# Windowed attention and soft mixture of experts on one core: three-row constants for the distance ramp, an earlier maximum in round 1, seven unused products

## The chip, the cores and the metric

The kernel runs on one core of a Trainium2 chip. The metric is the device time of one execution in microseconds. The core has five engines that run side by side, each with its own queue of instructions: TensorE (PE in the profile, with its weight loads listed apart as PEld), VectorE (DVE), ScalarE (ACT), GpSimd (POOL) and SyncE (SP), which here only issues transfers.

## The reference

Attention over a window of 128 positions with a penalty that grows with distance, then a soft mixture of experts over all tokens:

```python
# q, k, v: batch 8, heads 8, positions 576, head size 64
scores = scale * q @ k.T
bias = slopes * (-|i - j|)
scores = where((i - j >= 0) & (i - j < 128), scores + bias, -1e9)
attn = softmax(scores);  x = attn @ v            # 4608 tokens x 512
logits = x @ phi                                 # 32 slots: 8 experts x 4
slot_input = softmax(logits, over tokens).T @ x
slot_out = relu(slot_input @ w1[e]) @ w2[e]      # per expert, 512 -> 1024 -> 512
out = softmax(logits, over slots) @ slot_out
```

## The kernel before

**Rounds.** Attention is cut into 72 groups: per batch four tiles of 128 queries in two halves of the heads each, and a last tile of 64 queries in one piece. The loop over `i` (L726) is one round per group, and in a round the engines work on different groups. Everything stands under an order written out by hand, so each engine executes its instructions in the order of the code.

**Scores of a group** (`scores`, L235 on). Two banks of products are filled. The first four products (L252) write the distance ramp: a constant `pair_of` as weights against a constant `ramp` as moving operand, 384 columns in bf16. Only three of their rows hold anything; the operands have 64 rows each, of which 61 are zero, so that these products have the shape 64*64 (rows*columns of the array that they occupy) like the products of queries and keys after them. Those (L261) are fp32, sixteen in a round, and add on top of the ramp. Four of either kind sit in the four quarters of the array at the same time.

**Softmax of a group.** `merge` (L277, DVE) folds the two windows into one by a mask, `rowmax` (L291, DVE) takes the negated maximum, `bias` (L295, DVE) scales it, `expo` (L354, ACT) makes the four exponentials with their sums, `total` (L300) adds a small constant to the sums (on POOL, in round 2 on DVE), `inverse` (L304, DVE) takes the reciprocal, `normalise` (L308, DVE) multiplies. `softmax_front(new, old)` orders this for the group whose scores have just come and the group before it.

**After that.** `flip` (L369, PE, shape 64*128) transposes the normalised weights, `split` (L375 ACT, L381 and L383 POOL) copies and masks them, `values` (L405, PE, shape 128*64) multiplies with v, `x_store` (L419, DVE) copies out; `x_flip` (L428), `logits` (L446) and what follows feed the mixture. In round `i` PE has: flip of an older group, values of a still older one, scores of group `i+1`, then pieces of the mixture. `scores(i+1)` overwrites the bank that `expo(i-1)` read and waits for it.

**The first rounds differ.** Round 0 has only scores and softmax, in two halves. In round 1, `softmax_front` treats group 0 as `first`: the total (POOL) and the reciprocal (DVE) of group 0 come ahead of the maximum of group 1, half of the normalising is done on ACT (`normalise_first`, L313) and half on DVE. The first flip of weights is that of group 0, in round 2, after `scores(2)`.

**The start.** Six warm-up products (L225, 512 columns of bf16) run on a zeroed tile while the first loads are under way. SP issues keys of tile 0 (L185), then, once DVE has cleared `ramp` and `pair_of` (L204, L205), four small transfers of constants (L217, L218), and later the other loads; ACT issues the three first loads of queries (L181). A transfer's semaphore is one of eight, given out in turn, so the ninth transfer is issued when the first has landed.

Of the kernel before, what the change touches and what calls it, by code (L numbers as in the profile page):

```python
# [10 lines left out]
F32 = mybir.dt.float32  # L11
F32R = mybir.dt.float32r
BF16 = mybir.dt.bfloat16
# [11 lines left out]
P = 128  # L25
# [10 lines left out]
WIN = P + KB  # L36
# [7 lines left out]
FLAG = 3  # L44
# [15 lines left out]
def slide(ap):  # L60
    return bass.AP(ap.tensor, ap.offset, [list(ap.ap[0]), [KB, 2], [1, WIN]])
# [10 lines left out]
def tile_attn_softmoe(  # L72
# [13 lines left out]
    nc = tc.nc  # L86

    cpool = ctx.enter_context(tc.tile_pool(name="cpool", bufs=1))
# [16 lines left out]
    ln = lne[:, :, 0:NS]  # L105
    acc = cpool.tile([P, DM], F32, name="acc")
    kq = cpool.tile([P, 3 * UW], F32, name="kq")
    ramp = cpool.tile([P, 2, 2 * P], BF16, name="ramp")
    pair_of = cpool.tile([P, 2, P], BF16, name="pair_of")
    area = cpool.tile([P, 20, HW], F32, name="area")  # L110

    kall = kq[:, 0:NPAIR * S].rearrange("p (n j w) -> p n j w", n=NB, j=NPAIR)
    qs = [kq[:, NPAIR * S + 2 * P * i:NPAIR * S + 2 * P * i + 2 * P] for i in range(3)]
    half = [slice(64 * par, 64 * par + 64) for par in range(2)]

    def halves(i):
        return area[:, i].rearrange("p (u w) -> p u w", u=4)
# [25 lines left out]
    st = {}  # L143
# [54 lines left out]
    v_taken = []  # L198

    with tc.manual_schedule(engines=ORDERED):  # L200
        warm = area[:, 2].bitcast(BF16)[:, 0:512]
        nc.vector.memset(warm, 0.0)
        nc.vector.memset(low, LOW)
        nc.vector.memset(ramp, 0.0)  # L204
        nc.vector.memset(pair_of, 0.0)  # L205
        nc.vector.memset(fine[:, 10:11], -1.0)
        nc.gpsimd.memset(mask, 1.0)
        for c in range(2):
            rows = slice(KB * c, KB * c + KB)
            nc.gpsimd.affine_select(  # L210
                mask[rows, 0], mask[rows, 0], [[-1, KB]], ALU.is_ge, 0.0, base=0, channel_multiplier=1)
            nc.gpsimd.affine_select(
                mask[rows, 1], mask[rows, 1], [[1, KB]], ALU.is_gt, 0.0, base=0, channel_multiplier=-1)
        load_k(0, 0)
        load_q(0, nc.scalar)
        for par in range(2):
            nc.sync.dma_start(ramp[64 * par:64 * par + 3], slopes[par, :, 2 * P:])  # L217
            nc.sync.dma_start(pair_of[64 * par:64 * par + 3], slopes[par, :, 0:2 * P])  # L218
        load_q(1, nc.scalar)
        load_q(2, nc.scalar)  # L220
        load_k(0, 1)
        tiny = work.tile([P, 1], F32, tag="nm", name="tiny")
        nc.scalar.activation(tiny, low, AF.Exp)
        for i in range(WARM):
            nc.tensor.matmul(free[i % 4], lhsT=warm[:, 0:P], rhs=warm, start=True, stop=True)  # L225
        nc.gpsimd.memset(lgm, LOW)
        nc.gpsimd.memset(lne[:, :, NS:NS + 1], EPS)
        nc.gpsimd.memset(area[:, 3, 0:P], 1.0)
        nc.gpsimd.affine_select(
            unit_r, area[:, 3, 0:P], [[1, P]], ALU.is_equal, 0.0, base=0, channel_multiplier=-1)  # L230
        load_v()
        nc.scalar.dma_start(cst[:, P:], cstd)
        nc.scalar.dma_start(phi, phid)
        for t in range(2, NT):
            load_k(0, t)  # L235

    def scores(i):
        b, t, g = groups[i]
        if i == 0:
            parts = [pq[:, 0], ps_1.tile([P, 4 * P], F32, tag="xp", name="s4_0")]  # L240
        else:
            parts = [s4s[i % 2][:, 2 * par:2 * par + 2].rearrange("p u w -> p (u w)") for par in range(2)]
        qt = qs[i % 3].rearrange("p (j w) -> p j w", w=width(t))
        second = WIN if t < 4 else 2 * P
        for par, rows in enumerate(half):
            if t < 4:
                dst, src = parts[par][:, 0:2 * WIN], slide(ramp[rows, g])
            else:
                dst, src = parts[par].rearrange("p (u w) -> p u w", u=2)[:, :, 0:WIN], ramp[rows, :, 0:WIN]
            for jj in range(2):  # L250
                strip = slice(KB * jj, KB * jj + KB)
                nc.tensor.matmul(  # L252
                    dst[strip], lhsT=pair_of[rows, int(t == 0), strip], rhs=src, start=True, stop=False)
        for u in range(2):
            h, hp = (u, g) if t < 4 else (0, u)
            skip = max(2 * (1 - t) - h, 0)
            m0 = 2 * (t - 1) + h
            for par, rows in enumerate(half):
                for jj in range(2):
                    j = 2 * hp + jj  # L260
                    nc.tensor.matmul(  # L261
                        parts[par][KB * jj:KB * jj + KB, second * u + KB * skip:second * u + WIN],
                        lhsT=qt[rows, jj if t < 4 else j, KB * h:KB * h + KB], rhs=kall[rows, m0 + skip:m0 + 3, j],
                        start=False, stop=(u == 1))
        st[groups[i]] = {"parts": parts, "s4": s4s[i % 2].rearrange("p (a u) w -> p a (u w)", a=2)}
# [31 lines left out]
    def total(key, us, eng=None):  # L297
        if "rs" not in st[key]:
            st[key]["rs"] = work.tile([P, 4], F32, tag="rs", name="rs", bufs=3)
        (eng or nc.vector).tensor_scalar(  # L300
            st[key]["rs"][:, us], st[key]["sm"][:, us], EPS, 1.0, op0=ALU.add, op1=ALU.mult)

    def inverse(key, us):
        nc.vector.reciprocal(st[key]["rs"][:, us], st[key]["rs"][:, us])  # L304

    def normalise(key, us):
        p4, rs = st[key]["p4"][:, us], st[key]["rs"][:, us]
        nc.vector.tensor_tensor(p4, p4, bc(rs, 2, P), op=ALU.mult)  # L308

    def normalise_first(key, us):  # L310
        p4 = st[key]["p4"]
        for u in range(4)[us]:
            nc.scalar.mul(p4[:, u], p4[:, u], st[key]["rs"][:, u:u + 1])  # L313

    fillers = []

    def filler():
# [3 lines left out]
    def softmax_front(new, old):  # L321
        first, eager = number[old] == 0, 0 < number[old] < EAGER
        late = number[new] > SKIP
        if number[new] > SKIP + 1:
            normalise(groups[number[old] - 1], ALL)
        merge(new)
        filler()
        if not eager:
            total(old, ALL, nc.gpsimd)
        if first:  # L330
            inverse(old, ALL)
            normalise_first(old, LO)
        rowmax(new, ALL)
        filler()
        if not first and not eager:
            inverse(old, ALL)
        filler()
        bias(new, ALL)
        if eager:
            total(old, ALL)  # L340
            inverse(old, ALL)
        filler()
        if not late or number[new] == n - 1:
            normalise(old, HI if first else ALL)

    def expo(key, us=ALL):
        s = st[key]
# [11 lines left out]
    def flip(key, us=ALL, to=None, pair=None):  # L359
        s = st[key]  # L360
        if to is not None:
            s["pt"] = to.rearrange("p u (r w) -> p u r w", r=2)
            for u in range(4)[us]:
                nc.tensor.transpose(to[:, 2 * (u % 2) + u // 2], s["p4"][:, u], ident)
            return
        s["pt"] = (pq_p if pair is None else pair).rearrange("p r (u w) -> p u r w", u=4)
        for u in range(4)[us]:
            for r, rows in enumerate(half):
                nc.tensor.transpose(s["pt"][:, 2 * (u % 2) + u // 2, r], s["p4"][rows, u], ident[rows, rows])  # L369
# [350 lines left out]

    turn, ready = [0], {}

    with tc.manual_schedule(engines=ORDERED):
        scores(0)
        loads(0)
        for i in range(n):  # L726
            new = groups[i]
            run("pre", i)
            if i:
                softmax_front(new, groups[i - 1])  # L730
            else:
                for us in (LO, HI):
                    merge(new, us)
                    rowmax(new, us)
                    bias(new, us)
                    expo(new, us)
            near = int(i < SKIP)
            if i + near >= FLAG and i != SKIP:
                flip(groups[i + near - FLAG])
                split(groups[i + near - FLAG])  # L740
            run("act", i)
            if i + near >= LAG and i != SKIP:
                values(groups[i + near - LAG])
                after_values(i, groups[i + near - LAG])
            if i + 1 < n:
                scores(i + 1)
            if i + 1 < n - 1:
                loads(i + 1)
            if i == n - 1:
                run("pe", i)  # L750
                x_keep(last, 2)
            if i:
                expo(new)
            run("pe", i)
            load_weights_at(i)
            run("dve", i)
# [321 lines left out]
```

## Time and profile before

| | us |
|---|---|
| median of 3 runs (lowest, highest) | 277.69 (276.69, 278.99) |
| the profiled execution, whole | 277.36 |
| its span, first to last instruction | 275.4 |
| PE busy | 253.3 (92%) |
| VectorE busy | 214.4 (78%) |
| ScalarE busy | 189.5 (69%) |
| GpSimd busy | 108.5 (39%) |
| mean granted clock of TensorE, share of full | 0.979 |

Busy shares are means over stages: the start (to about 18 us), the attention rounds (to about 212 us) and the experts with the output (to the end). Matmuls are pipelined, so that the distance from the start of one block of products to the start of the next says more than the printed durations. The chain of the profile is the sequence of work that ended last, followed backwards.

### The profile page before, as it was taken

To read this page: it belongs to the slowest core of one execution; us is meant where nothing else is said; L and a number is where in the kernel's file an instruction comes from. 1 tells how busy PE (TensorE), PEld (TensorE's weight loads), DVE (VectorE), ACT (ScalarE), POOL (GpSimd) and SP (SyncE) were. 2 spreads that over 40 slices of the span, in tenths; PEclk is the share of its full clock that TensorE was granted. 3 is DMA by queue.
4 is the path that set the end of the run, shared out by engine and by line. 5 is a ranking of instruction groups with operands and counts; after the bars stand their busy time and mean duration, and the time that the engine had idled before them with its cause. 6 is when DMAs were issued, how large, how long until landed. Compare 5 with 4: busy or idle time off the path is not lost.

```text
span 275.4 us, 11691 instructions
## 1 busy us (share of the span) xinstructions
PE 253.3 (92%) x4589; PEld 176.5 (64%) x4589; DVE 214.4 (78%) x549; ACT 189.5 (69%) x778; POOL 108.5 (39%) x221
## 2 busy tenths in 40 slices
PE   6599999989999999899998999999999899999980
PEld 2366676767667677667766766667767433777750
DVE  2779998997997899699799899789896556674450
ACT  2868878897897788778888889778977301154450
POOL 3025735480675276328526551656755001000000
PEclk9779999999999999999999999999999999999996
DMA  6834557888897979887879988787577799977997
GB/s 167 291 88 144 156 165 254 257 285 275 256 304 250 308 238 309 278 273 233 270 239 335 315 266 275 270 283 221 160 256 236 244 334 384 408 282 257 332 362 273
DMA packets 36478, 72.49 MB, mean 263 GB/s; under 512 B 4380, under 2 KB 14792, under 8 KB 36424
## 3 DMA queue, kind: packets, MB, share of 16 engines
q1 hardware_dynamic: 35704, 71.25, 77.9%
q8 instruction: 36, 0.59, 0.9%
q10 hardware_dynamic: 720, 0.51, 0.6%
q14 instruction: 18, 0.15, 0.2%
HBM read 62.30 MB, written 9.44 MB: 261 GB/s over the span
## 4 chain that ended last, share of the span: by engine, by line
PE 59%; DVE 15%; ACT 11%; POOL 6%; issue 5%; DMA 2%; ACTq 0%; POOLq 0%; DVEq 0%
PE xp L405 14%; PE s L261 9%; ACT area L354 8%; PE op L917 5%; PE hp L878 5%; PE pq L369 4%; PE s L252 4%; DVE s L291 4%; PE lp L446 4%; DVE area L308 4%; PE po L942 3%; POOL area L383 3%; PE pq L428 3%; DVE s L277 2%; POOL area L381 2%
## 5 line engine op out<-in xcount | busy, mean ns | idle before, releaser
L354 ACT ACTIVATE area<-s,nb 128x128 f32<-128x128 f32 x286 | 101.9, 378 | 24.6 <-DVE nb L295 22.6
L405 PE MATMUL xp<-area 128*64 128x128 f32 (+1 forms) x1104 | 72.9, 271 | 2.3 <-POOL area L383 1.7
L354 ACT ACTIVATION_READ_ACCUMULATOR area<-s,nb 128x1 f32 x286 | 61.9, 216 | 0.0
L405 PEld LDWEIGHTS xp<-area 128*64 128x64 f32 x1104 | 54.2, 137 | 9.9 <-POOL area L383 5.0
L308 DVE TENSOR_TENSOR area<-area,rs 128x512 f32<-128x512 f32 (+1 forms) x73 | 58.1, 796 | 0.6
L261 PE MATMUL s<-kq 64*64 64x192 f32 (+2 forms) x1144 | 56.2, 311 | 1.0 <-issue 0.8
L291 DVE TENSOR_REDUCE s<-s 128x4 f32<-128x512 f32 (+1 forms) x72 | 50.0, 694 | 2.2
L375 ACT COPY area<-pq 128x512 f32<-128x512 f32 (+1 forms) x72 | 42.5, 593 | 10.4 <-PE pq L369 8.9
L383 POOL TENSOR_SCALAR_AFFINE_SELECT area<-area 128x512 f32<-128x512 f32 (+1 forms) x57 | 45.4, 797 | 3.9
L381 POOL TENSOR_SCALAR_AFFINE_SELECT area<-area 128x512 f32<-128x512 f32 (+1 forms) x57 | 37.7, 662 | 21.8 <-ACT area L375 20.7
L300 POOL TENSOR_SCALAR rs<-sm 128x4 f32<-128x4 f32 x70 | 15.0, 215 | 77.4 <-ACT area L354 71.4
L261 PEld LDWEIGHTS s<-kq 64*64 64x64 f32 x1144 | 39.4, 135 | 5.1 <-issue 1.1
L369 PE MATMUL pq<-unit_r,area 64*128 64x64 f32 x560 | 31.9, 233 | 3.2 <-ACT area L313 2.2
L277 DVE COPY_PREDICATED s<-cst,s 128x256 f32<-128x256 int32 (+1 forms) x72 | 30.1, 418 | 2.4 <-PE s L261 2.4
L369 PEld LDWEIGHTS pq<-unit_r,area 64*128 64x128 f32 x560 | 23.4, 140 | 13.2 <-issue 3.9
L419 DVE COPY area<-xp 128x512 f32<-128x512 f32 (+1 forms) x38 | 24.2, 636 | 6.4 <-PE xp L405 5.9
L252 PE MATMUL s<-ramp,pair_of 64*64 64x384 bf16 x286 | 26.1, 350 | 3.3 <-ACT area L354 2.4
L437 ACT COPY area<-pq 128x512 f32<-128x512 f32 x34 | 20.4, 600 | 0.6 <-PE pq L428 0.6
L428 PEld LDWEIGHTS pq<-unit_r,area 64*128 64x128 f32 x272 | 11.0, 137 | 14.6 <-issue 12.1
L252 PEld LDWEIGHTS <-pair_of 64*64 64x64 bf16 x288 | 9.3, 103 | 16.1 <-issue 11.8
L428 PE MATMUL pq<-unit_r,area 64*128 64x64 f32 x272 | 15.7, 234 | 0.6 <-ACT area L375 0.4
L944 ACT COPY ob<-po 128x512 f32<-128x512 f32 x20 | 11.3, 587 | 6.1 <-PE po L942 5.6
(145 smaller groups left out, 264.5 us busy)
## 6 DMA issues: line engine op xcount, KB each, us to landing
w<-w SPq DMA_DIRECT2D x53, 512.0 KB, 5.5
out<-ob SPq DMA_DIRECT2D x36, 256.0 KB, 3.5
kq<-q_t SPq DMA_DIRECT2D x69, 128.0 KB, 3.9
area<-v_n SPq DMA_DIRECT2D x33, 256.0 KB, 5.1
kq<-k_t SPq DMA_DIRECT2D x32, 256.0 KB, 4.1
area<-w SPq DMA_DIRECT2D x8, 512.0 KB, 7.1
kq<-w SPq DMA_DIRECT2D x3, 512.0 KB, 6.8
kq<-k_t SPq DMA_DIRECT2D x8, 128.0 KB, 3.9
```

What stands on the lines that cost most here:

```text
L252: nc.tensor.matmul(dst[strip], lhsT=pair_of[rows, int(t == 0), strip], rhs=src, start=True, stop=False)
L261: nc.tensor.matmul(parts[par][KB * jj:KB * jj + KB, second * u + KB * skip:second * u + WIN], lhsT=qt[rows, jj if t < 4 else j, KB * h:KB ...
L277: nc.vector.copy_predicated(to, keep, of)
L291: nc.vector.tensor_reduce(st[key]["mx"], merged(key, us), axis=AX.X, op=ALU.max, negate=True)
L308: nc.vector.tensor_tensor(p4, p4, bc(rs, 2, P), op=ALU.mult)
L354: nc.scalar.activation(s["p4"][:, u], src, AF.Exp, bias=s["nb"][:, u:u + 1], scale=SCALE, accum_out=s["sm"][:, u:u + 1],)
L369: nc.tensor.transpose(s["pt"][:, 2 * (u % 2) + u // 2, r], s["p4"][rows, u], ident[rows, rows])
L375: nc.scalar.copy(pa[:, us].rearrange("p u (r w) -> p u r w", r=2), s["pt"][:, us])
L381: nc.gpsimd.affine_select(prev, own, [[-step, m], [0, 4], [-1, KB]], ALU.is_gt, 0.0, base=-i0, channel_multiplier=1)
L383: nc.gpsimd.affine_select(own, own, [[step, m], [0, 4], [1, KB]], ALU.is_ge, 0.0, base=i0, channel_multiplier=-1)
L405: nc.tensor.matmul(xp[D * par:D * par + D, j, 0:w], lhsT=v_slot[b, t - 1 + ph][:, D * h:D * h + D], rhs=src[:, :, par, i] if t < 4 else sr ...
L428: nc.tensor.transpose(xq[:, j, r], x[rows, j], ident[rows, rows])
```

## The change

- One tile `slp` takes the place of `ramp` and `pair_of`. The constants are loaded into rows 0 to 2 and 64 to 66 with one transfer each, issued as the first transfers of SP and of ACT, ahead of the keys and queries; the two clearing memsets and the four transfers behind them go. The ramp's products use these three rows alone (`three[par]`) in place of 64, in every round.
- In round 1 the maximum and `bias` of group 1 come ahead of the reciprocal of group 0, and DVE does the whole normalising of group 0; `normalise_first` goes.
- Six products without use run on PE ahead of the first flip of weights (in round 2) and one behind it, from the zeroed tile of the warm-up, which moves from `area[:, 2]` to `area[:, 15]` so that it is still there.

```diff
-    ramp = cpool.tile([P, 2, 2 * P], BF16, name="ramp")
-    pair_of = cpool.tile([P, 2, P], BF16, name="pair_of")
+    slp = cpool.tile([P, 6 * P], BF16, name="slp")
+    pair_of = slp[:, 0:2 * P].rearrange("p (a w) -> p a w", a=2)
+    ramp = slp[:, 2 * P:].rearrange("p (a w) -> p a w", a=2)
...
+    three = [slice(64 * par, 64 * par + 3) for par in range(2)]
...
-        warm = area[:, 2].bitcast(BF16)[:, 0:512]
+        for par, eng in enumerate((nc.sync, nc.scalar)):
+            eng.dma_start(slp[three[par]], slopes[par])
+        warm = area[:, 15].bitcast(BF16)[:, 0:512]
...
-        nc.vector.memset(ramp, 0.0)
-        nc.vector.memset(pair_of, 0.0)
...
-        for par in range(2):
-            nc.sync.dma_start(ramp[64 * par:64 * par + 3], slopes[par, :, 2 * P:])
-            nc.sync.dma_start(pair_of[64 * par:64 * par + 3], slopes[par, :, 0:2 * P])
...
-                dst, src = parts[par][:, 0:2 * WIN], slide(ramp[rows, g])
+                dst, src = parts[par][:, 0:2 * WIN], slide(ramp[three[par], g])
...
-                    dst[strip], lhsT=pair_of[rows, int(t == 0), strip], rhs=src, start=True, stop=False)
+                    dst[strip], lhsT=pair_of[three[par], int(t == 0), strip], rhs=src, start=True, stop=False)
...
-        if first:
-            inverse(old, ALL)
-            normalise_first(old, LO)
         rowmax(new, ALL)
...
         if eager:
             total(old, ALL)
+        if eager or first:
             inverse(old, ALL)
         filler()
         if not late or number[new] == n - 1:
-            normalise(old, HI if first else ALL)
+            normalise(old, ALL)
...
+    def busy(k):
+        to = ps_1.tile([P, 512], F32, tag="mi", name="busy")
+        for _ in range(k):
+            nc.tensor.matmul(to, lhsT=warm[:, 0:P], rhs=warm, start=True, stop=True)
...
+                if i + near == FLAG:
+                    busy(6)
                 flip(groups[i + near - FLAG])
+                if i + near == FLAG:
+                    busy(1)
```

More of the change, by code (lines that the diff above doesn't have):

```diff
@@ L246, in scores @@
             if t < 4:
-                dst, src = parts[par][:, 0:2 * WIN], slide(ramp[rows, g])
+                dst, src = parts[par][:, 0:2 * WIN], slide(ramp[three[par], g])
             else:
-                dst, src = parts[par].rearrange("p (u w) -> p u w", u=2)[:, :, 0:WIN], ramp[rows, :, 0:WIN]
+                dst, src = parts[par].rearrange("p (u w) -> p u w", u=2)[:, :, 0:WIN], ramp[three[par], :, 0:WIN]
             for jj in range(2):
@@ L308, in normalise @@
         nc.vector.tensor_tensor(p4, p4, bc(rs, 2, P), op=ALU.mult)
[L310 to L313, printed above, removed]
     fillers = []
```

## The prediction

> **What bounds the kernel now.** I read the page first: engines' shares and the chain that ended last.
>
> ```profile
> PE 253.3 (92%) x4589; PEld 176.5 (64%) x4589; DVE 214.4 (78%) x549; ACT 189.5 (69%) x778; POOL 108.5 (39%) x221
> PE 59%; DVE 15%; ACT 11%; POOL 6%; issue 5%; DMA 2%; ACTq 0%; POOLq 0%; DVEq 0%
> ```
>
> PE sets most of the chain. Next the stages: a stretch, its length, busy us (and instructions) of PE, PEld, DVE, ACT and POOL in it, the granted clock, the DMA share and GB/s.
>
> ```profile
> 18.15:33.42 15.27, 13.37 (x262) 9.90 (x264) 14.81 (x35) 12.41 (x55) 10.23 (x17) 1.00 0.51 146
> 33.00:212.00 179.00, 173.66 (x3371) 126.10 (x3369) 159.38 (x406) 147.85 (x644) 93.37 (x182) 1.00 0.81 260
> ```
>
> Up to 33 us DVE is the bound (14.81 of 15.27). From there to the end of attention PE works 173.66 of 179.00 us, so it is idle for 5.3 us in 61 rounds (72 groups, of which 11 have their scores before that): anything that lengthens PE's part of a round goes almost whole into the time.
>
> The start is another matter. The chain in order of time, from the first exponentials to those of group 1:
>
> ```profile
> 7.86 0.82 ACT area L354 x4
> ...
> 8.75 0.20 POOL rs L300
> ...
> 9.16 0.60 DVE s L291
> ...
> 9.78 0.17 DVE nb L295
> ...
> 10.06 1.52 ACT area L354 x8
> ```
>
> The maximum of group 1 (9.16) stands behind POOL's total of group 0, which ends at 8.95, and the reciprocal that needs it. And TensorE's granted clock, in windows of 3.41 us:
>
> ```profile
> 4.15:7.57 3.42, 2.50 (x60) 1.67 (x60) 1.52 (x5) 0.57 (x3) 0.00 (x0) 1.00 0.71 184
> 7.57:10.98 3.41, 0.89 (x12) 0.61 (x9) 2.43 (x9) 2.66 (x13) 0.19 (x1) 1.00 0.94 303
> 10.98:14.39 3.41, 2.77 (x32) 2.00 (x33) 2.43 (x7) 2.76 (x14) 0.19 (x1) 0.50 0.68 248
> 14.39:17.81 3.42, 3.42 (x40) 2.17 (x38) 2.00 (x6) 2.04 (x10) 0.19 (x1) 0.50 0.40 115
> ```
>
> After a window in which PE did 0.89 us of work the clock is 0.50 for two windows. The rounds in them show it; these are the first scores of rounds from PE's timeline:
>
> ```profile
> 5.28 0.30 PE L261 MATMUL pq<-kq 64*64 64x64 f32 x3
> 9.80 0.87 PE L369 MATMUL pq<-unit_r,area 64*128 64x64 f32 x8 [2.15 <-ACT area L313]
> 11.62 0.53 PE L252 MATMUL s<-ramp,pair_of 64*64 64x384 bf16 x4 [0.95 <-ACT area L354]
> 15.03 0.53 PE L252 MATMUL s<-ramp,pair_of 64*64 64x384 bf16 x4
> 18.15 0.36 PE L252 MATMUL s<-ramp,pair_of 64*64 64x384 bf16 x4
> 21.20 0.36 PE L252 MATMUL s<-ramp,pair_of 64*64 64x384 bf16 x4
> 23.80 0.36 PE L252 MATMUL s<-ramp,pair_of 64*64 64x384 bf16 x4
> ```
>
> So the change works on two places: the first 18 us, where it removes waits, and the four ramp products of every round, on the engine that is the bound.
>
> **The change part by part.** All terms are against the profiled execution: 277.36 us whole, span 275.4. It lies 0.3 below the median of the runs, 277.69.
>
> *Constants loaded first: -0.75 us.*
>
> ```profile
> 2.46 0.27 SPq L218 DMA_DIRECT2D pair_of<-slopes  x1
> 0.79 1.37 ACTq L181 DMA_DIRECT2D kq<-q_t  x3
> 0.79 3.30 DMA kq<-q_t
> ```
>
> The last of four constants is issued at 2.46, and the scores that need it go on at 5.28, 2.8 us later at most. Issued at 0.79 they would be there by 3.6, before the warm-up products end. What is late next is the first queries: they landed at 0.79 + 3.30 = 4.1, and on ACT's queue they now stand behind one transfer of constants, 1.37 / 3 = 0.46 us, so about 4.5 in place of products that begin at 5.28. Keys shift by as much on SP. I take 0.75. Two fewer transfers also let the keys of tile 1 and the first values go earlier, since the ninth transfer no longer is one of them. Against that, the DMA share of 0.94 at 7.57 says that the queries of group 3 may then be the late ones, so the term is 0.35 to 0.95. The memsets that go are DVE work before 1.6 us, under the loads: nothing.
>
> *Round 1's maximum first: -1.05 us.* The fold of group 1 ends at 8.10 (7.68 + 0.42):
>
> ```profile
> 7.68 0.42 DVE L277 COPY_PREDICATED s<-cst,s 128x256 f32<-128x256 int32 x1
> 9.08 0.67 DVE L291 TENSOR_REDUCE s<-s 128x4 f32<-128x512 f32 x1
> 12.02 0.69 DVE L308 TENSOR_TENSOR area<-area,rs 128x512 f32<-128x512 f32 x1
> ```
>
> The maximum (0.67 for this width) then runs from 8.10, the scaling (0.17) ends at 8.95, ACT has been free since 8.68, and group 1's exponentials start at 9.0 where they started at 10.06. They end 1.05 earlier, and the scores at 11.62, which wait for them, follow. The reciprocal still waits for POOL's total and ends by 9.16 as now, and the whole normalising on DVE (0.69) ends at 9.87, between the two halves of before, so the first flip isn't later than now. ACT loses 0.69 us of `normalise_first`. Range 0.8 to 1.06.
>
> *Seven products: -1.4 us.* The warm-up products are of the same size:
>
> ```profile
> 1.24 2.74 PE L225 MATMUL s<-area 128*128 128x512 bf16 x6 [1.24 <-DVE fine L203]
> ```
>
> Six take 2.74, and half of that, 1.4, if those ran at half clock (the clock column says 1.00 there, but nothing is recorded before them). PE is free for them from 7.65 until the flip: 1.4 fits beside other work; 2.7 would hold the flip up by 0.5. With them the window of 7.57 to 10.98 holds about 1.4 + 0.46 (flip) + 0.23 + 0.4 (scores, now at 10.57) = 2.5 us of PE instead of 0.89, and with 2.50 the window before it kept the clock. What that is worth: two rounds of 3.41 and 3.12 us. The next two, at full clock, took 3.05 and 2.60, which would give 0.9. But these have twice the values and POOL's masks in them; following flip, values and exponentials of the two rounds at full clock I get 2.6 and 2.1, which gives 1.8. I take 1.4; the bounds are nothing (clock falls all the same) and 3.1, half of PE's 6.19 us at half clock.
>
> *Three rows in place of 64: +5.4 us.* A dense round on PE's timeline:
>
> ```profile
> 34.28 0.46 PE L428 MATMUL pq<-unit_r,area 64*128 64x64 f32 x8
> 34.58 0.42 PE L369 MATMUL pq<-unit_r,area 64*128 64x64 f32 x8
> 34.93 1.09 PE L405 MATMUL xp<-area 128*64 128x128 f32 x16
> 35.95 0.36 PE L252 MATMUL s<-ramp,pair_of 64*64 64x384 bf16 x4
> 36.14 0.82 PE L261 MATMUL s<-kq 64*64 64x192 f32 x16
> 36.89 0.46 PE L369 MATMUL pq<-unit_r,area 64*128 64x64 f32 x8
> 37.28 1.15 PE L405 MATMUL xp<-area 128*64 128x64 f32 x32
> ```
>
> Sixteen transposes of one shape between two other shapes take 34.93 - 34.28 = 0.65, eight take 37.28 - 36.89 = 0.39. Eight more cost 0.26, so the two changes of shape cost 0.39 - 0.26 = 0.13: **one change of shape, leaving and entering, costs PE 0.13 us**. Between L252 and L261 there is none now: both are 64*64, and the fp32 products follow 0.19 us behind the first ramp product. With three rows the ramp has a shape of its own, so each round gets one change more. No row shows a 32-row shape next to a 64-row one, so its price lies between nothing and 0.13; I take 0.13, because every change in that round costs it, whether rows, columns or both change. The products themselves I cost at nothing: their columns stay, and in these rows the time goes by columns.
>
> How many of them reach the end? The chain lists the ramp's products as pieces like
>
> ```profile
> 33.42 0.29 PE s L252 x4
> 197.67 0.29 PE s L252 x4
> ```
>
> 35 of them from 33 us on: 35 x 0.13 = 4.6, which stays as long as the rest of that chain does. The other 26 of 61 rounds have PE waiting for DVE, ACT or POOL, and its 5.3 us of idle time covers most of their 26 x 0.13 = 3.4; I let a quarter through, 0.8. Before 33 us DVE covers it. So +5.4, with 4.6 and 61 x 0.13 = 7.9 as the ends, and nothing if a change to three rows is free.
>
> The Trainium skill, TensorEngine Tiling (Array Packing), section Key Properties, says that changing the tiling mode, not just the tile, drains the engine; its section Tiling Modes has 128, 64 and 32 rows as modes, and three rows fall in the last. By that rule every round pays, and the sum is the one below; were a mode of rows free, it would be 274.2. The trace agrees for the shapes that it has, with 0.13 us.
>
> **Sum:** 277.36 - 0.75 - 1.05 - 1.4 + 5.4 = **279.6 us**, 0.7% above the median. The rounds carry a gain of the start through: of the chain's 2% in DMA, 5.5 us, the first queries alone are 3.3, so hardly a load stands in it later on.
>
> **The rivals.**
>
> *A: the three-row products cost no change.* For it: the quarters of the array that they sit in are the same; against it: 0.13 at every change seen. 277.36 - 3.2 = 274.2, faster.
>
> *B: every round pays in full,* the slower side. PE's 5.3 us of idle time from 33 to 212 us cover nothing, because the engines that it waits for got their own input from PE and are late by as much: 277.36 + 7.9 - 3.2 = 282.1. It decides once the added 0.13 is no longer below a typical wait of those rounds, and 5.3 / 61 = 0.09 us a round is on its side; the chain's 26 rounds without the ramp speak against it.
>
> *C: the seven products don't hold the clock.* 2.5 us of PE work lies just at the 2.50 of the window that kept it, and the windows may fall otherwise against the program in another run. Then 1.4 are lost: 281.0. The Trainium skill, TensorE: Matmul & The Clock Gate, section Part 4, says that transposes don't count as activity in the same way. By that, the first flip's 0.46 wouldn't count and the window would hold 2.0, which makes C likelier; that a window with only the flip in it (0.87 of its 0.89) lost the clock agrees.
>
> **How the numbers follow.** Forecast 0.50, A 0.27, B 0.11, C 0.12. The forecast's own range, from its bounds, is 277.5 to 282. With A below it the range is 273.6 to 282.4: it leaves out the best start together with A, and B together with C. A measurement of this kernel tells about 1% from no change, so the borders are 274.9 and 280.5. Faster: 0.7 of A, 0.19. Slower: a third of the forecast, B, and 0.6 of C, 0.35. Within 1%: 0.46.
>
> **What would show it.** In the changed kernel's timeline of PE, a dense round: from the start of L252 to that of the shape behind L261 it is now 36.89 - 35.95 = 0.94 us; at 1.07 the change of shape is paid, at 0.94 A holds. L261 of group 0 should begin near 4.5, group 1's exponentials near 8.2, the clock should be 1.00 from the warm-up to the end of attention, and the scores of group 3 should begin near 9.8. A first flip held back by the unused products, or scores of group 3 that wait for their queries, would take from the start's 3.2 us. Wrong altogether it would be if the ramp's rows of three made PE's other products slower, for which nothing in this trace speaks.

## The result, and the profile after

| | median us (lowest, highest) |
|---|---|
| before, beside it | 276.88 (275.22, 279.77), 18 runs |
| after | 280.26 (278.23, 283.70), 18 runs |
| ratio after / before | **1.0112 [1.0083, 1.0141]**: 3.1 us slower |

Ratios leave out the slow executions, which lie more than 1.5% above the fastest of their kernel, so they are not quite the quotient of the medians. 279.6 was forecast, 0.7 below the measured median. The total came out, but two of its terms did not come as they were put, and most of what follows is about where these two hide. The profiled execution of after took 283.7 us (span 281.9): it has the clock at half for two windows in the experts' stage as well (222.8 to 229.6 us), which the profile of before has not there, so below only its stages before that are read.

The page's engine line and the chain's shares by engine, of after:

```profile
PE 266.1 (94%) x4596; PEld 175.8 (62%) x4596; DVE 213.8 (76%) x547; ACT 190.1 (67%) x776; POOL 108.5 (38%) x221
PE 75%; ACT 6%; POOL 5%; DVE 5%; issue 4%; DMA 2%; ACTq 1%; POOLq 0%; DVEq 0%
```

PE's share of the chain went from 59% to 75% with seven instructions more. So PE does not do more, each round of it takes longer. Windows of after (columns as before: length, busy of PE, PEld, DVE, ACT, POOL, clock, DMA share, GB/s):

```profile
4.35:7.76 3.41, 1.94 (x48) 1.04 (x48) 2.41 (x8) 1.48 (x8) 0.00 (x0) 1.00 1.05 350
7.76:11.18 3.42, 3.42 (x22) 1.43 (x20) 3.14 (x10) 1.64 (x10) 0.20 (x1) 0.50 0.79 255
11.18:14.59 3.41, 3.41 (x55) 1.95 (x53) 1.46 (x4) 2.47 (x10) 0.19 (x1) 1.00 0.42 140
33.00:212.00 179.00, 177.72 (x3317) 123.98 (x3317) 155.48 (x396) 147.25 (x638) 90.16 (x176) 1.00 0.80 257
```

Two things are to be seen. In the attention rounds PE is busy 177.72 of 179.00 us where it was 173.66, and got through 3317 products in place of 3371 in the same stretch. And the half clock is still there: one window of it, from 7.76, where there were two from 10.98. The window that lost it is the one ahead, and there PE had 1.94 us of work.

A dense round of after on PE's timeline:

```profile
34.39 1.09 PE L397 MATMUL xp<-area 128*64 128x128 f32 x16
35.41 0.35 PE L251 MATMUL s<-slp 3*64 3x384 bf16 x4
35.70 0.88 PE L260 MATMUL s<-kq 64*64 64x192 f32 x16
36.51 0.46 PE L361 MATMUL pq<-unit_r,area 64*128 64x64 f32 x8
```

L251 is the ramp, L260 the products of queries and keys, L361 the flip. From ramp to flip it is 36.51 - 35.41 = 1.10 us where it was 0.94. The fp32 products begin 0.29 behind the ramp (0.19 before) and take 36.51 - 35.70 = 0.81 (0.75 before): of the 0.16 more, 0.10 is waiting and 0.06 lies in the block behind. Ahead of the ramp nothing changed: from L397 to L251 it is 35.41 - 34.39 = 1.02, as it was from L405 to L252.

The start, PE's timeline of after, with the time that PE waited ahead of a block and for what in brackets:

```profile
4.50 0.27 PE L260 MATMUL pq<-kq 64*64 64x64 f32 x2
...
6.02 0.56 PE L260 MATMUL s<-kq 64*64 64x64 f32 x16 [0.67 <-DMA kq<-q_t]
...
7.62 1.47 PE L260 MATMUL s<-kq 64*64 64x192 f32 x16 [0.75 <-DMA kq<-q_t]
9.02 2.52 PE L718 MATMUL busy<-area 128*128 128x512 bf16 x6
11.47 0.46 PE L361 MATMUL pq<-unit_r,area 64*128 64x64 f32 x8
...
12.19 0.35 PE L251 MATMUL s<-slp 3*64 3x384 bf16 x4
```

Group 0's scores begin at 4.50 (5.28 before), but the next two groups wait 0.67 and 0.75 us for their queries. Before, no group waited for queries at this place; group 2 waited 0.25 us for keys:

```profile
6.77 0.88 PE L261 MATMUL s<-kq 64*64 64x192 f32 x16 [0.25 <-DMA kq<-k_t]
```

The queries of group 2 were issued at 1.7 us before and took 3.2 us to land; in after they are issued at 2.24, behind the constants on ScalarE's queue, and take 5.24. On SyncE's queue the first values (`v_n`) go 2.8 us earlier than before; first before, then after:

```profile
4.88 0.35 SPq L196 DMA_DIRECT2D area<-v_n  x1
```

```profile
2.09 0.43 SPq L198 DMA_DIRECT2D area<-v_n  x1
```

Only behind the scores of group 2 come the six unused products (L718), at half clock, and they hold the first flip until 11.47. The chain in order of time says the same, and has the unused products on it:

```profile
2.24 5.24 DMA kq<-q_t
7.49 0.14 issue
7.62 1.47 PE s L260 x16
9.09 2.45 PE busy L718 x6
11.54 0.39 PE pq L361 x8
```

On VectorE and ScalarE the new order did what it says:

```profile
8.50 0.69 DVE L307 TENSOR_TENSOR area<-area,rs 128x512 f32<-128x512 f32 x1
```

```profile
8.37 0.37 ACT L346 ACTIVATE area<-s,nb 128x128 f32<-128x128 f32 x1 [0.48 <-DVE nb L294]
```

Group 1's exponentials start at 8.37 (10.06 before), group 0 is normalised at 9.19. The flip that needs it could have begun there, 2.3 us before it did.

So that many kernels can be compared, here is the start of the first ramp product of some groups, in us from the start of the span, from PE's timeline of each profiled run. Group 10 marks the end of the start, 10 to 71 are the rounds in which PE is the bound.

| kernel | rows | group 3 | group 10 | group 71 | 10 to 71 |
|---|---|---|---|---|---|
| before | 64 | 11.62 | 30.78 | 203.46 | 172.7 |
| after | 3 | 12.19 | 30.08 | 206.67 | 176.6 |
| three rows only | 3 | 11.62 | 33.96 | 210.69 | 176.7 |
| three rows and seven products | 3 | 11.82 | 29.42 | 206.32 | 176.9 |
| 32 rows only | 32 | 12.16 | 30.95 | 207.58 | 176.6 |
| 33 rows only | 33 | 11.55 | 30.70 | 201.71 | 171.0 |
| after with 64 rows | 64 | 12.73 | 30.45 | 201.71 | 171.3 |
| ... and loads paced | 64 | 10.75 | 28.71 | 199.34 | 170.6 |
| after with 64 rows, without the seven products | 64 | 10.66 | 30.09 | 201.31 | 171.2 |
| maximum first only | 64 | 10.82 | 29.02 | 200.25 | 171.2 |
| seven products only | 64 | 11.64 | 28.77 | 200.27 | 171.5 |
| both of these | 64 | 10.99 | 28.37 | 200.04 | 171.7 |
| both, and three rows | 3 | 13.48 | 31.10 | 207.69 | 176.6 |
| constants first only | 64 | 11.98 | 30.73 | 201.92 | 171.2 |

The last column falls into two sets, 170.6 to 172.7 and 176.6 to 176.9, and what tells them apart is the rows alone: up to 32 rows, or 33 and more. (Before's 172.7 holds one wait of some 1.2 us near 116 us that no other kernel shows.)

### The profile page after: what moved, and what is told of

The parts are those of the page before. It is cut to its first block, busy times and chain, and to the rows that moved or that the text cites. A ratio compares the mean times of both kernels' runs of the same rounds, so it can differ in the third digit from the quotient of the medians.

```text
span 281.9 us, 11697 instructions
## 1 busy us (share of the span) xinstructions
PE 266.1 (94%) x4596; PEld 175.8 (62%) x4596; DVE 213.8 (76%) x547; ACT 190.1 (67%) x776; POOL 108.5 (38%) x221
## 4 chain that ended last, share of the span: by engine, by line
PE 75%; ACT 6%; POOL 5%; DVE 5%; issue 4%; DMA 2%; ACTq 1%; POOLq 0%; DVEq 0%
PE xp L397 18%; PE s L260 14%; PE pq L361 6%; PE hp L879 6%; PE op L918 5%; PE s L251 5%; ACT area L346 5%; PE pq L420 3%; PE lp L438 3%; PE po L943 3%; PE ap L505 3%; POOL area L375 3%; POOL area L373 2%; DMA kq<-q_t 2%; DVE s L290 1%
## 5 line engine op out<-in xcount | busy, mean ns | idle before, releaser
L397 PE MATMUL xp<-area 128*64 128x128 f32 (+1 forms) x1104 | 71.6, 269 | 1.4 <-POOL area L375 0.8
L260 PE MATMUL s<-kq 64*64 64x192 f32 (+2 forms) x1144 | 59.0, 321 | 1.4 <-DMA kq<-q_t 1.4
L397 PEld LDWEIGHTS xp<-area 128*64 128x64 f32 x1104 | 53.7, 136 | 8.1 <-POOL area L375 3.3
L307 DVE TENSOR_TENSOR area<-area,rs 128x512 f32<-128x512 f32 (+1 forms) x73 | 57.1, 782 | 0.8
L375 POOL TENSOR_SCALAR_AFFINE_SELECT area<-area 128x512 f32<-128x512 f32 (+1 forms) x57 | 46.8, 821 | 3.9
L373 POOL TENSOR_SCALAR_AFFINE_SELECT area<-area 128x512 f32<-128x512 f32 (+1 forms) x57 | 37.2, 652 | 23.4 <-ACT area L367 22.3
L260 PEld LDWEIGHTS s<-kq 64*64 64x64 f32 x1144 | 34.3, 133 | 14.9 <-issue 12.8
L361 PE MATMUL pq<-unit_r,area 64*128 64x64 f32 x560 | 31.1, 230 | 0.9 <-DVE area L307 0.7
L361 PEld LDWEIGHTS pq<-unit_r,area 64*128 64x128 f32 x560 | 22.9, 138 | 10.4 <-issue 6.1
L251 PE MATMUL s<-slp 3*64 3x384 bf16 x286 | 25.7, 346 | 0.8 <-ACT area L346 0.8
L879 PE MATMUL hp<-w,acc 128*8 128x512 f32 (+1 forms) x128 | 17.1, 688 | 0.0
L251 PEld LDWEIGHTS <-slp 3*64 3x64 bf16 x288 | 8.4, 101 | 13.2 <-issue 9.2
L420 PE MATMUL pq<-unit_r,area 64*128 64x64 f32 x272 | 15.7, 235 | 0.1
```

The lines of the kernel that those rows point to most:

```text
L251: nc.tensor.matmul(dst[strip], lhsT=pair_of[three[par], int(t == 0), strip], rhs=src, start=True, stop=False)
L260: nc.tensor.matmul(parts[par][KB * jj:KB * jj + KB, second * u + KB * skip:second * u + WIN], lhsT=qt[rows, jj if t < 4 else j, KB * h:KB ...
L373: nc.gpsimd.affine_select(prev, own, [[-step, m], [0, 4], [-1, KB]], ALU.is_gt, 0.0, base=-i0, channel_multiplier=1)
L375: nc.gpsimd.affine_select(own, own, [[step, m], [0, 4], [1, KB]], ALU.is_ge, 0.0, base=i0, channel_multiplier=-1)
L397: nc.tensor.matmul(xp[D * par:D * par + D, j, 0:w], lhsT=v_slot[b, t - 1 + ph][:, D * h:D * h + D], rhs=src[:, :, par, i] if t < 4 else sr ...
L420: nc.tensor.transpose(xq[:, j, r], x[rows, j], ident[rows, rows])
```

## The experiments

Ratios are to before, timed on the same chip, with 95% intervals.

**Three rows only.** Before, with the ramp's products cut to their first three rows; nothing else is changed.

```diff
-        for par, rows in enumerate(half):
+        for par in range(2):
+            rows = slice(64 * par, 64 * par + 3)
```

> The kernel before with one edit: the ramp's products take 3 rows of the same zero-padded tiles, loads and all else as before. Theory (a change of shape at every round): in a dense round the stretch from the start of L252 to the shape behind L261 goes from 0.94 to 1.10 us, and the whole is 4 to 6 us slower (1.4 to 2.2%), since 59 rounds pay 0.16 us and a third of it falls into PE's waits. Rival (the slowdown of the change came from its start, and the three rows cost nothing): 0.94 stays and the time is within 0.3% of before.

284.83 us, ratio 1.0325 [1.0301, 1.0349]. This one edit costs more than the whole change, 9.0 us by the ratio, and more than the 4 to 6 us expected. In the profiles, 4.0 us more lie in the rounds from group 10 on (5.7 against the 33-row kernel, which lacks before's stray wait) and 3.2 in the start. Its windows show what differs in the start:

```profile
7.93:11.35 3.42, 0.81 (x8) 0.61 (x9) 2.47 (x7) 2.72 (x13) 0.19 (x1) 1.00 1.00 332
11.35:14.76 3.41, 3.14 (x34) 2.00 (x35) 2.22 (x7) 2.56 (x12) 0.19 (x1) 0.50 0.50 181
14.76:18.17 3.41, 3.41 (x38) 1.94 (x36) 1.79 (x6) 1.83 (x10) 0.19 (x1) 0.50 0.40 113
18.17:21.59 3.42, 3.42 (x38) 1.95 (x36) 2.88 (x7) 1.90 (x9) 1.86 (x3) 0.50 0.14 38
21.59:25.00 3.41, 3.41 (x36) 2.34 (x36) 1.40 (x4) 2.00 (x9) 1.80 (x3) 0.50 0.41 123
25.00:28.41 3.41, 3.00 (x60) 2.15 (x53) 2.94 (x7) 2.41 (x10) 1.68 (x2) 1.00 0.26 77
```

Four windows at half clock with PE busy 3.14 to 3.42 us in each, where before had two.

**32 and 33 rows.** The same edit with 32 and with 33 in place of 3.

> As the one with 3 rows, with 32 rows of the same tiles (29 of them zero). Theory (32 rows or fewer are another shape for the array, whatever their number): as with 3 rows, stretch 1.10 us, 1.4 to 2.2% slower. Rival (the price comes from how few rows are fed): about half of the price of 3 rows, stretch near 1.0 us.

> As the one with 32 rows, with 33 (30 of them zero). Theory (33 rows need the 64-row shape that L261 has, so nothing changes between them): stretch 0.94 us, within 0.3% of before. Rival (any difference in rows between the two is a change): as with 32 rows, 1.10 us and 1.4 to 2.2% slower.

32 rows: 284.13 us, 1.0298 [1.0256, 1.0340], again more than expected. 33 rows: 276.62 us, 1.0012 [0.9978, 1.0046]. Not all of the 8.2 us of 32 rows is the price of the rounds: in its profile 4.0 lie between groups 10 and 71 (5.6 against 33 rows) and 1.9 behind them, where one window of the experts' stage, from 223.9 us, has the clock at half. First a round of the 32-row kernel, then one of the 33-row kernel:

```profile
36.28 0.35 PE L253 MATMUL s<-ramp,pair_of 32*64 32x384 bf16 x4
36.57 0.88 PE L262 MATMUL s<-kq 64*64 64x192 f32 x16
37.38 0.46 PE L370 MATMUL pq<-unit_r,area 64*128 64x64 f32 x8
```

```profile
35.87 0.36 PE L253 MATMUL s<-ramp,pair_of 33*64 33x384 bf16 x4
36.06 0.82 PE L262 MATMUL s<-kq 64*64 64x192 f32 x16
36.81 0.46 PE L370 MATMUL pq<-unit_r,area 64*128 64x64 f32 x8
```

1.10 us against 0.94, with one row between them. So it is neither the few rows nor the odd number: 3 and 32 rows cost the same 0.16 us, 33 cost nothing, as 64 do. The reading is that up to 32 rows the product is of another shape than the block behind it and from 33 on it isn't; whether 32-row products next to others of 32 rows would be free, no run here tests. The Trainium skill, TensorEngine Tiling (Array Packing), section Key Properties, says that a change of tiling mode drains the engine while a change of tile within a mode doesn't, and its section Tiling Modes names 64 and 32 rows as separate modes. These two runs agree, with 0.16 us for the change that 32 rows bring.

**After with 64 rows.** All of the change but the rows. The tile is cleared first, as it needs zeros in the other rows, so the two transfers go 0.56 us later (1.35 in place of 0.79).

```diff
+        nc.vector.memset(slp, 0.0)
...
-                dst, src = parts[par][:, 0:2 * WIN], slide(ramp[three[par], g])
+                dst, src = parts[par][:, 0:2 * WIN], slide(ramp[half[par], g])
```

> The changed kernel with the ramp's products on 64 rows again: the one tile is cleared by DVE first, and its two transfers are still the first, some 0.4 us later. Theory: the changed kernel without its price per round, so some 4 to 5 us faster than it; against before only the start's gain is left, 0 to 1 us as the changed kernel's start shows it, ratio 0.995 to 1.00; the stretch is 0.94 us. Rival (the start is what costs): it stays 1% slower than before.

274.59 us, 0.9955 [0.9925, 0.9984]. The rest of the change gives 1.2 us, not the 3.2 of the sum, and the rows cost 1.0112 - 0.9955, 4.3 us, in medians; 176.59 - 171.26 = 5.3 us between groups 10 and 71 of the two profiles. Group 0's products begin at 5.30 here, 0.45 us of it a wait for their own queries, so this kernel does not have the early start that after has (4.50).

**The parts of the start, one at a time.** The new order of round 1 alone; the seven products alone (and the zeroed tile moved); then three rows with the seven products, and after with 64 rows but without them.

```diff
-        if first:
-            inverse(old, ALL)
-            normalise_first(old, LO)
...
+        if eager or first:
             inverse(old, ALL)
...
-            normalise(old, HI if first else ALL)
+            normalise(old, ALL)
```

> The kernel before with the order of round 1 alone changed (maximum of group 1 ahead of the reciprocal of group 0, all of the first normalising on DVE). Theory (the term of the prediction was right where nothing else is in the way): group 1's exponentials start 1.05 us earlier, the scores of group 3 begin at 10.6 instead of 11.62, and the time is 0.5 to 1 us shorter (ratio 0.996 to 0.998). Rival (what follows is bound by the half clock and the flip, so it is given back): 0.998 to 1.002.

```diff
+                if i + near == FLAG:
+                    busy(6)
                 flip(groups[i + near - FLAG])
+                if i + near == FLAG:
+                    busy(1)
```

> The kernel before with the seven products without use alone, 64 rows, start as before. Theory of the prediction: scores of group 2 end at 7.65, six products run to 9.0 at full clock, the first flip is not held, the clock isn't halved at 11, and by the scores of group 6 the kernel is 1.4 us ahead (0 to 3.1): ratio 0.990 to 1.00. Rival (seen in the changed kernel, where they ran at half clock for 2.5 us and the flip waited): the flip starts 0.5 to 1.5 us later and the gain is below 0.5 us.

> The kernel before with 3 rows and the seven products. The run with 3 rows alone had the clock at half for four windows of 3.41 us (11.35 to 25.0) where before had two, and was 3.2 us behind by the scores of group 10, ahead of any price per round. Theory (the three-row products keep the clock down for longer at the start, and the products without use lift it): no half clock after 15 us, 2.5 to 4 us faster than with 3 rows alone, ratio to before 1.017 to 1.025. Rival (the longer half clock was chance of that one run): ratio stays at 1.03 to 1.035.

> The changed kernel with 64 rows and without the seven products. Theory (they hold the first flip up by some 2 us, since queries come late and the clock is at half, but spare the half clock after it): the flip starts near 10 instead of 12.0, the clock stays at half for one or two windows more, and the time comes out within 0.4% of the one with them. Rival (they only cost): 1 to 2 us faster than with them. Rival (they are worth what the prediction said): 1 to 2 us slower.

The order alone: 275.57 us, 0.9966 [0.9929, 1.0003], -0.9 us, with an interval that just includes no change. The seven products alone: 275.19 us, 0.9940 [0.9908, 0.9972], -1.7 us. Windows of that kernel around its first flip:

```profile
7.32:10.74 3.42, 2.83 (x31) 1.32 (x23) 2.44 (x9) 2.68 (x14) 0.19 (x1) 1.00 0.97 307
10.74:14.15 3.41, 2.55 (x45) 1.80 (x48) 3.21 (x10) 3.23 (x16) 0.19 (x1) 1.00 0.78 270
```

The clock stays at 1.00 where before had 0.50. With three rows they help more, 281.96 us, 1.0187 [1.0131, 1.0242] in place of 1.0325, and the profile has one window at half clock in place of four. But in after with 64 rows they are worth nothing that can be told: without them it takes 275.22 us, 0.9944 [0.9911, 0.9976], against 0.9955 with them.

So these two terms were sized about right, each by itself, and yet after with 64 rows, which has both and the early constants too, gains only 1.2. What is left as a suspect is the third part.

**Both without the early constants, and these alone.** Before with the order and the seven products, 64 rows and its own loads; and before with the one tile `slp`, cleared and loaded first (and the zeroed tile moved).

```diff
+        nc.vector.memset(slp, 0.0)
+        for par, eng in enumerate((nc.sync, nc.scalar)):
+            eng.dma_start(slp[three[par]], slopes[par])
...
-        nc.vector.memset(ramp, 0.0)
-        nc.vector.memset(pair_of, 0.0)
...
-            nc.sync.dma_start(ramp[64 * par:64 * par + 3], slopes[par, :, 2 * P:])
-            nc.sync.dma_start(pair_of[64 * par:64 * par + 3], slopes[par, :, 0:2 * P])
```

> The kernel before with 64 rows and its own loads, with the order of round 1 and the seven products of the change together. Alone they gave 0.9966 and 0.994. Theory (they work on different things, one on the first exponentials, one on the clock): they add up, ratio 0.989 to 0.992, so some 1.2 us better than with the change's loads on top (0.9955). Rival (they shorten the same gap on PE): 0.993 to 0.996.

> The kernel before with 64 rows and the constants loaded first in one cleared tile, without the new order of round 1 and without the seven products. Theory (the first scores come earlier, but keys of tile 1 and the first values now travel beside the queries of groups 1 and 2 and make them late, so it is given back by group 2): ratio 0.998 to 1.002, scores of group 2 later than 6.8 us. Rival (the prediction's term): scores of group 2 at 6.0, ratio 0.996 to 0.998.

Both without the early constants: **273.72 us, 0.9905 [0.9873, 0.9937]**, 2.6 us faster than before, the sum of the two parts (0.9 + 1.7). Constants first alone: 276.09 us, 0.9986 [0.9953, 1.0020], nothing that can be told. Added to the other two they give back 0.9955 - 0.9905, 1.4 us (0.2 to 2.6 from the two intervals). In the two kernels with early constants that these figures rest on, the tile is cleared first, and group 0's products begin at 5.28 (constants alone) and 5.30 (after with 64 rows), as in before: what is measured here is the lateness without the early start of after. The scores of group 2 in the constants-first kernel, and the first flip in the kernel with both:

```profile
8.08 0.88 PE L261 MATMUL s<-kq 64*64 64x192 f32 x16 [1.00 <-DMA kq<-q_t]
```

```profile
8.64 1.48 PE L724 MATMUL busy<-area 128*128 128x512 bf16 x6
10.26 0.47 PE L367 MATMUL pq<-unit_r,area 64*128 64x64 f32 x8
```

With the early constants PE waits 1.00 us for the queries of group 2, and starts their products at 8.08; without them the six products ahead of the flip begin at 8.64, at full clock, and the flip at 10.26, where after has 9.02, half clock and 11.47.

**Loads paced.** If early keys and values crowd out the queries, holding these loads back must bring the gain. After with 64 rows, with the first values and the keys of tiles 2 to 4 issued behind the fourth queries (each of the first rounds issues one load of values; now four do, as the one ahead of them goes):

```diff
-        load_v()
...
-        for t in range(2, NT):
-            load_k(0, t)
...
-        if i < 3:
+        if i < 4:
...
         loads(0)
+        for t in range(2, NT):
+            load_k(0, t)
```

> The changed kernel with 64 rows, and with the first values and the keys of tiles 2 to 4 issued only behind the fourth queries, which wait for the first scores, so that less travels beside the first queries. Theory (the late queries of groups 1 and 2 are what gives the start's gain back): no wait for queries over 0.3 us, the first flip before 10.8 instead of 12.0, ratio 0.987 to 0.991. Rival (the start is bound by the half clock, whatever the queries do): 0.994 to 0.997, as without the pacing.

273.76 us, 0.9912 [0.9878, 0.9946]: 1.2 us faster than the same kernel unpaced (-0.1 to 2.4 from the two intervals). PE's timeline, unpaced first, then paced:

```profile
6.31 0.56 PE L261 MATMUL s<-kq 64*64 64x64 f32 x16 [0.28 <-DMA kq<-q_t]
...
8.16 1.54 PE L261 MATMUL s<-kq 64*64 64x192 f32 x16 [1.12 <-DMA kq<-q_t]
10.04 2.04 PE L719 MATMUL busy<-area 128*128 128x512 bf16 x5 [0.33 <-DVE area L308]
12.01 0.46 PE L362 MATMUL pq<-unit_r,area 64*128 64x64 f32 x8
```

```profile
6.28 0.57 PE L258 MATMUL s<-kq 64*64 64x64 f32 x16 [0.35 <-DMA kq<-q_t]
...
7.59 1.47 PE L716 MATMUL busy<-area 128*128 128x512 bf16 x6
10.03 0.46 PE L359 MATMUL pq<-unit_r,area 64*128 64x64 f32 x8 [0.98 <-DVE area L305]
```

The queries of group 2 are issued at 2.81 in both kernels and land after 5.2 us unpaced, after 3.8 paced, so what travels beside them delays them. How late they are varies: the unpaced kernel without the seven products, the same up to there, waited 0.39 in place of 1.12. Paced, this wait is gone (one of 0.35 for group 1 stays, against at most 0.3 expected), the unused products run at 7.59 at full clock, take 1.47 in place of 2 and more, and fit into PE's idle time: the flip now waits for VectorE, not for them.

**Both, and three rows.** What the rows cost on top of the kernel with both parts. This is also after without its early constants.

> The kernel with the new order of round 1 and the seven products, loads as before (0.9905 of before with 64 rows), now with 3 rows in the ramp's products. Theory (each round that PE bounds pays 0.16 us, about 33 of 61 pay it all, and the clock is held by the seven products): 5 to 5.5 us on top of it, ratio to before 1.008 to 1.012. Rival (as with 3 rows in the kernel before, where the half clock lasted longer): 8 to 9 us on top of it, 1.020 to 1.025. Rival (every one of 61 rounds pays): 9.8 us on top, 1.026.

281.52 us, 1.0181 [1.0142, 1.0220]. The price is 7.6 us (1.0181 - 0.9905 of 276.2), between the two expectations, so neither theory had it whole. The rounds from group 10 to 71 took 176.59 against 171.67 us, 4.9 more, as the price of a change of shape has it. The other 2.7 came before group 10 (31.10 against 28.37). There the clock was lifted later, as PE's timeline shows by the length of known blocks:

```profile
10.05 2.34 PE L725 MATMUL busy<-area 128*128 128x512 bf16 x5 [0.34 <-issue]
12.32 0.69 PE L368 MATMUL pq<-unit_r,area 64*128 64x64 f32 x8
```

The flip takes 0.69 at 12.32 us and the five products 2.34, both at half clock; in the kernel with both and 64 rows, six such products took 1.48 at 8.64 and the flip 0.47.

Set beside after, this run says more. With three rows the early constants are worth 1.0181 - 1.0112, 1.9 us (0.6 to 3.3 from the two intervals), where with 64 rows and a cleared tile they cost 1.4. After has them 0.56 us earlier than those 64-row kernels. In its profile the clock is at full from 4.35 to 7.76 and again from 11.18, and group 10 comes at 30.08 in place of 31.10.

## Why the prediction came out, point by point

- **Three rows: right in size for the rounds, by two errors that cancel.** It had 5.4; the profiles show 5.3 (after against 64 rows) and 4.9 (the last pair) between groups 10 and 71. A change costs 0.16 a round, not 0.13, because the block behind it starts late and also runs 0.06 longer. And more of it is hidden: 61 x 0.16 = 9.8, of which 5.3 arrive, 54%; the sum let 5.4 of 7.9 through, 68%. The 35 rounds with the ramp on the chain would give 35 x 0.16 = 5.6 by themselves. What would show it was named as 1.07 against 0.94; it is 1.10. What the term left out is the start ("Before 33 us DVE covers it"): the whole price of three rows is 9.0 us in before, 7.6 with both parts, 6.8 with the seven products alone and 4.3 in after, and up to group 10 it is 3.2, 2.7, 0.7 and -0.4.
- **Round 1's maximum first: the mechanism right, the size in line.** -1.05 forecast, -0.9 measured alone (interval -2.0 to 0.1). Group 1's exponentials were to start near 8.2 and start at 8.37.
- **Seven products: right alone, not in after with 64 rows.** -1.4 forecast, -1.7 measured alone. In after with 64 rows they are worth nothing that can be told. The profile of after shows how they can cost what they save: they start at 9.02, at half clock, take 2.5 us and stand ahead of a flip whose input is there at 9.19. The sum had the case, "2.7 would hold the flip up by 0.5", but it took PE to be free from 7.65.
- **Constants loaded first: the step that failed.** Group 0's products began at 4.50 in after, as forecast. But the step "Two fewer transfers also let the keys of tile 1 and the first values go earlier" was booked as a gain, and it makes the queries of groups 1 and 2 late, since these transfers now travel beside them; the prediction feared this for group 3 alone. What the lateness is worth in time depends on the rest. With 64 rows, where the cleared tile also takes the early start away, it is 0 alone and 1.4 us given back beside the other two parts. With three rows, as in after, the early constants gain 1.9 us all the same, more than the 0.75 forecast. Why they gain there isn't shown; after's clock was at full from 4.35, that of the kernel without them only from 13.56.
- **The sum.** With the rows taken last: start -3.2 forecast, -1.2 measured; rows +5.4 forecast, +4.3 in medians (3.2 to 5.5, from the two intervals). With the constants taken last it is -2.6 for the other two parts, +7.6 for the rows, -1.9 for the constants. The parts do not simply add, and only their total is sure: +2.2 forecast, +3.1 measured. That 279.6 lies so near 280.26 is luck in part: the forecast started from 277.36, 0.5 above before's median. Its own range, "277.5 to 282", isn't what its bounds add up to, which is 276.9 to 284.1; the measured time lies in both. And the 0.13 is called the price of "the two changes of shape" once and of one the next moment; from the start of a block to the start of the next there is one. "The clock should be 1.00" and "the scores of group 3 should begin near 9.8" both failed (0.50 from 7.76, 12.19), and showed where to look.
- **Rivals.** A (a change is free) falls with the 32- and the 33-row kernels. B (every round pays in full) falls: 5.3 of 9.8 in the rounds. C (the products don't hold the clock) happened in the profiled run of after, but otherwise than it was put: the clock was lost in the window ahead of them, in which PE waited 0.67 and 0.75 us for queries. Whether transposes count less for the clock, which C cited, no run here tests.

**Open:** three rows cost 3.2 us in the start of one kernel and 2.7 in another, and both times the clock was lifted later; with the seven products alone it was 0.7, and in after nothing. Whether products of three rows count for less in what lifts or holds the clock, or the windows merely lay otherwise against the work in those runs, these runs don't tell: each has one profile, and the first lift that these record lies anywhere from 3.9 to 15.7 us. One pair speaks for the first. In the two kernels that add the seven products to before, one with three rows and one with 64, the windows begin within 0.08 us of each other; with three rows PE has 2.56 us of work in the window and the clock falls, with 64 rows 2.08 and it stays (the window from 7.32 is shown above):

```profile
3.99:7.40 3.41, 2.56 (x52) 1.47 (x56) 1.15 (x5) 0.20 (x1) 0.00 (x0) 1.00 0.76 210
7.40:10.81 3.41, 3.41 (x22) 0.99 (x11) 2.46 (x8) 2.66 (x13) 0.19 (x1) 0.50 0.92 308
```

```profile
3.91:7.32 3.41, 2.08 (x53) 1.47 (x56) 1.24 (x5) 0.29 (x2) 0.00 (x0) 1.00 0.68 207
```

Some profiles (after, 32 rows, three rows with the seven products, constants first) have one or two windows at half clock in the experts' stage, between 218 and 230 us, and the others have none there. One of these four kernels has 64 rows; what decides it no run tests.

## What to carry to other kernels

Padding an operand with zero rows can be what makes it cheap: ahead of cutting it, look at the shapes on either side in the timeline, and count the changes of shape per round on the engine that is the bound. A transfer taken out of the front of a queue moves up all that stand behind it, and these then share the bandwidth with the loads that are urgent: check the next waits, not only the one that goes. Work put in to keep the clock up pays while it ends before the next real work is ready, so it has to be placed by the clock at which it will run; parts are to be measured together as well as alone, since one that costs in one company can gain in another.

## What the runs showed of the hardware that was not expected

- **A window with PE more than half busy can lose the clock.** In after the window 4.35 to 7.76 has 1.94 of 3.41 us busy, and the next is at 0.50; with 2.55 and 2.83 (seven products alone) it was kept. Busy time alone doesn't decide: the pair shown under Open lost it with 2.56 and kept it with 2.08. The Trainium skill, TensorE: Matmul & The Clock Gate, section Part 1, ties the return to half clock to at least one idle window of about 3.4 us. The length agrees with the windows here; that the window must be idle does not.
- **The column of the granted clock says nothing ahead of its first record.** In the kernel with both parts, group 2's products and the window that they lie in:

```profile
7.04 1.68 PE L261 MATMUL s<-kq 64*64 64x192 f32 x16
```

```profile
5.29:8.70 3.41, 3.41 (x59) 2.71 (x54) 2.42 (x8) 1.49 (x8) 0.00 (x0) 1.00 0.92 276
```

1.00 by the column, and yet 1.68 us for sixteen products that take 0.82 at full clock (the 33-row round above). Durations of a known block tell the clock better than the column there.

- **Two windows of PE at 3.41 and 3.42 busy, with three-row products among the rest, did not lift the clock** (the kernel with three rows only, 14.76 to 21.59); it came back behind the third, at 25.00. In before it came back behind the first window that was as full (3.42, from 14.39 to 17.81).
